# Renumbering the PSUM banks of a fused attention and gated MLP kernel, with a new order of its steps

## The chip, the core and the metric

One NeuronCore of a Trainium2 chip runs the whole program. The metric is device time in microseconds (us) of one execution; the kernel before takes 639.93 us (median of 3 runs, 639.92 to 640.62). Five engines work from queues of their own and meet only at semaphores: TensorE (PE; its weight loads are shown as PEld), VectorE (DVE), ScalarE (ACT), GpSimd (POOL) and SyncE (SP), which issues most DMAs.

## What is computed

For 8 batches and 8 heads (576 positions, head size 64), causal attention by blocks of 64, then a gated MLP over each batch:

```python
scores = q @ k.T / sqrt(64);  scores = where(block_i >= block_j, scores, -1e9)
attn = exp(scores - max);  attn = attn / (sum(attn) + 1e-9);  x = attn @ v      # heads side by side: 576 x 512
h = relu(x @ w_in);  u, v = h[..., :512], h[..., 512:]
v_n = (v - mean(v)) / sqrt(var(v) + 1e-6)
v_s = w_spatial @ v_n + b_spatial
out = (u * v_s) @ w_out
```

Everything is fp32 in and out. Most matmuls are done as three products of rounded parts (high by high, high by low, low by high), so that each fp32 product costs three fast matmuls.

## The kernel before

**Steps.** The program is written as generators that yield after each small piece, a *step*; nearly every step is one instruction on one engine, or one burst of matmuls. A long string, `ORDER` (lines 46 to 155), names which generator is advanced next (`s.17*8` advances the scores of pair 17 eight times). `in_order` (lines 397 to 410) ties each instruction to the one before it on the same engine, so the string fixes the order in every engine's queue; between engines only data and buffers decide.

**Kinds of steps.** Two heads make a pair; there are 32 pairs g, four to a batch b. For each pair: `8.g` (`scores_8`, line 705) computes the scores of the last 64 rows, two PSUM banks, 64 by 64 in the array; DVE reduces each bank with its maximum (line 652, both into the one buffer `p8`), ACT takes the exponential, POOL normalises, `t8.g` (line 839) transposes on DVE. `s.g` (`scores_run`, line 781) computes the other four row tiles t = 3, 2, 1, 0 of both heads in one burst that needs six banks (t = 1 and 0 share one), 64 rows by 128 columns; DVE reduces them (line 593), ACT and POOL follow, `t.g` transposes (line 849, 8 instructions), `r.g` regroups by DMA. `a.g` (`av_pair`, line 882) multiplies with v in two halves z of one bank each, 128 rows by 64 columns; ACT copies each half out (line 506) and DVE subtracts for the low part (line 508), which frees the bank. For each batch the MLP has five `v` groups (12 or 8 matmuls), eight `u`, eight `g` (the spatial product) and fourteen `o` (the output product in seven products of halves), all over the full 128 by 128 array. `h` and the later steps of `g` prepare operands of `o` on ACT and POOL. Pairs 0 to 4 are treated apart in the opening (`set`, `ns`, `ts`, `alo`, `ahi`), where `w` and `sw` also load and split the weights; from `8.5` on the pairs of batch b + 1 run between the MLP groups of batch b.

**PSUM banks.** Eight banks: two (`ps_m`) for `v`, `u`, `g` and `o` with n = 0, six for the pairs: three in pool `s`, two in `t`, one in `av`. `bank` (line 580) picks the pool by a number modulo six, `RING` (line 578), and the pool hands out its buffer that came free first. A pair owns ten numbers: 0 to 5 its `s` banks, 8 and 9 the `8` banks of the next pair, and 6 and 7 the `a` banks of the pair before it (`16 + z` counted from that pair). So the numbers assume the sequence s.(g-1), a.(g-2), 8.g, s.g. The output groups with n = 1 and n = 3 take numbers 4 and 5 of pairs 4b + 7 and 4b + 8, which the scores of these pairs use too.

**Order around the change.** The order before goes to the narrow matmuls of a pair twice, once for `8.g` with both halves of `a.(g-2)` before or behind it, and once, a few wide groups later, for `s.g`.

Of the kernel before, what the change touches and what calls it, by code (L numbers as in the profile page):

```python
# [52 lines left out]
ts.10*2 set.14*2 ns.11 alo.1 ns.11*3 w.4 set.12 ts.10*2 alo.1 ns.12*2 loadv.2 ns.11 ts.9*2
ts.8*2 set.14*3 set.13*5 sw.1 ahi.1 ahi.2*3 w.5 w.6*3 ns.13 set.15*6 ns.13*2 ts.11*4 ns.14*3
ts.12 ahi.2*2 pad ahi.0 load.4 set.16*3 alo.2 loadv.3 set.15*2 ts.12*3 alo.2*2 w.4*3 set.15
ts.13*4 ts.14*4 ns.15*5 load.5 w.5*3 set.16*3 set.17*5 set.18*2 sw.1 ns.16*2 w.6*3 ahi.3*3 ts.15
ahi.2 ts.15*3 ns.17*3 set.19 set.18*3 alo.3*2 ns.16 8.5 set.19*5 ahi.3*3 set.19*3 w.6 w.7*3 t8.4
sw.4*2 alo.3 v.0.0*2 ns.18*3 t8.4 ns.19*3 t.4*3 w.8*3 ns.19 v.0.0*2 load.6 t.4*3 ns.19 t.4*2
# [12 lines left out]
n.8*4 a.7 n.8*5 loadv.8 o.0.3.1 n.8 t8.8*2 r8.8 8.9*3 o.0.4.0*2 o.0.2.1 o.0.4.1 o.0.3.1 o.0.4.1  # L71
a.7*3 8.9*2 o.0.5.0*3 t.8*2 load.10 split.9 o.0.6.0*2 t.8*5 n.8 t.8 r.8 v.1.0*4 o.0.6.1*3 a.5
o.0.5.1*3 a.4 a.7 a.6 v.1.4*2 v.1.0*2 split.9*2 v.1.0*2 8.9*3 s.9*11 v.1.4 v.1.1*2 v.1.4*5
u.1.0.1*2 v.1.1*2 n.9*4 u.1.0.0*2 s.9*5 t8.9*2 n.9*2 s.9 n.9 o.0.6.0 n.9*3 t.9*4 split.10*2 n.9
t.9*4 8.10 a.8*7 v.1.4*3 v.1.2*2 8.10*5 u.1.0.2*2 split.10 v.1.1*4 v.1.3*2 loadv.9 o.0.1.0
v.1.2*3 s.10*5 u.1.0.3*2 8.10*3 v.1.3*3 s.10*3 u.1.1.1*2 s.10*8 v.1.2 u.1.1.0 n.10*6 s.10 n.10*3
r8.9 t8.10*2 load.11 8.11*3 o.0.4.1 v.1.2*2 u.1.1.0 n.10*2 t.10*6 v.1.3*3 r.9 a.9*6 split.11*3
t.10*2 u.1.1.2*2 u.1.1.3*2 g.1.0.0*2 8.11*3 loadv.10 s.11*12 g.1.0.0*2 g.1.0.1*2 r8.10 g.1.0.1*2
o.0.4.0 s.11*5 8.11*3 g.1.0.2*4 load.12 split.12 g.1.1.0*3 n.11*5 g.1.0.3*4 t8.11*2 loadv.11
n.11*6 r.10 a.10*2 split.12*2 a.10*2 t.11*8 8.12 g.1.1.0 g.1.1.1*3 g.1.1.2*7 a.10 8.12*5 a.10  # L80
g.1.1.3*3 o.1.0.1*2 o.1.1.1*2 o.1.0.0*2 o.1.1.0*2 g.1.1.3*6 g.1.1.1 h.1.1 o.1.1.0 s.12*4 load.13
g.1.1.0 r8.11 h.1.0 s.12*9 g.1.1.1 s.12*2 g.1.1.2*2 o.1.2.1*2 o.1.2.0*2 8.12*3 n.12*4 s.12
# [6 lines left out]
s.14*5 u.2.0.3*2 s.14*3 v.2.3*3 n.14*2 v.2.4*3 s.14 n.14 s.14*2 n.14*2 s.14 n.14*4 u.2.1.0
n.14*2 t8.14*2 load.15 8.15*3 t.14*8 u.2.1.0 v.2.2*3 r.13 a.13*6 u.2.1.1*2 v.2.3*3 u.2.1.2*2  # L90
u.2.1.3*2 loadv.15 split.15*3 g.2.0.0*4 8.15*6 g.2.0.1*3 r8.14 g.2.0.1 s.15*9 g.2.0.2*4 n.15*5
s.15*2 g.2.0.3*4 s.15*6 n.15*4 g.2.1.0*3 load.16 split.16*2 8.16 t8.15*2 r.14 a.14*2 o.1.4.0
a.14*2 r8.15 t.15*4 split.16 t.15*2 n.15*2 t.15*2 g.2.1.1*3 g.2.1.2*7 a.14 g.2.1.3*3 o.2.0.1*2
g.2.1.2 o.2.0.0*2 g.2.1.0*2 8.16*5 g.2.1.3*6 o.2.1.1*2 g.2.1.1*2 o.2.1.0*3 a.14 s.16*10 g.2.1.2
o.2.2.0*2 8.16*2 n.16*4 8.16 s.16*6 o.2.1.1 h.2.0*4 o.2.2.1*2 h.2.1*4 o.2.3.0 r.15 a.15*2 t.16
a.15*2 t8.16*2 load.17 8.17*4 a.15*2 o.2.3.1 o.2.4.1 o.2.3.1 o.2.4.1 o.2.3.0 o.2.4.0*2 n.16 s.16
n.16*6 t.16*4 o.2.4.0 t.16*3 8.17*3 o.2.6.1*2 o.2.6.0*2 o.2.5.0*3 loadv.16 load.18 split.17*3
a.13 8.17*2 o.2.5.1*3 v.3.0*4 a.14 s.17*7 r8.16 a.15 a.12 v.3.4*2 s.17*8 loadv.18 o.2.6.1 v.3.1
s.17*2 v.3.4*4 v.3.0*4 u.3.0.0*2 v.3.4*2 n.17*4 t8.17*2 8.18 r.16 a.16*2 n.17*3 v.3.1*3 t.17
split.18 n.17*4 t.17*3 a.16*2 t.17*4 r8.17 u.3.0.1*2 u.3.0.2*2 v.3.4*3 v.3.2*2 8.18*5 split.18*2  # L100
# [1249 lines left out]
```

## Time and profile before

| | |
|---|---|
| median of 3 runs | 639.93 us |
| profiled execution | 640.71 us, its span 638.9 us |
| PE busy | 629.6 us, 99% of the span, 5380 matmuls |
| DVE, POOL, ACT busy | 78%, 67%, 66% |
| granted TensorE clock | 0.999 of full, all 40 slices at 9 tenths or more |

The span runs from the first to the last instruction; the remaining 1.8 us of the profiled execution lie around it. A matmul's end is modelled and matmuls overlap, so PE busy time says that PE is occupied, not how well; the distance from the start of one group to the start of the next says what a group costs. An idle time in brackets at the end of a row is what the engine waited before it, with the instruction that ended the wait.

### The profile page before, as it was taken

The numbers are of one execution on the slowest core, as the hardware profiler recorded it, in microseconds if no ns is written. First come the engines' busy times: TensorE is split into PE (matmuls) and PEld (weight loads), VectorE is DVE, ScalarE is ACT, GpSimd is POOL, SyncE is SP. The second block draws the span as 40 slices with busy tenths as digits, with TensorE's granted clock in tenths as the row PEclk, the third lists the DMA queues.
The fourth block names the chain that finished last, engine by engine and source line by source line (L and its number), as shares of the span: only waits on it lengthen the run. The fifth ranks groups of instructions, "written<-read, shape, count | busy, mean of one in ns | idle before, by whom it ended". The sixth has DMA issues, their size and how long they took to land.

```text
span 638.9 us, 15873 instructions
## 1 busy us (share of the span) xinstructions
PE 629.6 (99%) x5380; PEld 547.2 (86%) x5380; DVE 501.3 (78%) x1847; ACT 424.4 (66%) x1214; POOL 428.6 (67%) x690
## 2 busy tenths in 40 slices
...
PEclk9999999999999999999999999999999999999999
...
GB/s 273 208 130 219 177 133 197 134 147 158 142 175 134 183 162 158 90 206 114 155 205 129 156 159 105 165 194 158 143 81 223 107 208 123 135 123 47 10 1 84
DMA packets 51109, 93.47 MB, mean 146 GB/s; under 512 B 5970, under 2 KB 27986, under 8 KB 51028
## 3 DMA queue, kind: packets, MB, share of 16 engines
...
q14 instruction: 39, 0.32, 0.1%
...
## 4 chain that ended last, share of the span: by engine, by line
PE 87%; DVE 7%; DMA 2%; ACT 1%; POOL 1%; issue 1%; SPq 0%; DVEq 0%; POOLq 0%
PE ms L1082 15%; PE mo L1162 15%; PE mu L1030 14%; PE mv L947 12%; PE av L894 10%; PE s L801 7%; PE s L619 2%; PE av L906 2%; PE mv L959 2%; DMA raw<-qk 2%; DVE p L593 2%; PE t L453 1%; PE ms L1087 1%; PE ms L1086 1%; PE s_first L763 1%
## 5 line engine op out<-in xcount | busy, mean ns | idle before, releaser
L598 ACT ACTIVATE p<-p,sst 128x256 f32<-128x256 f32 (+2 forms) x240 | 132.1, 553 | 14.4 <-DVE sst L593 10.7
L695 POOL TENSOR_SCALAR p<-p,sst 128x256 f32<-128x256 f32 (+4 forms) x244 | 128.0, 543 | 18.3 <-DVE sst L691 4.8
L1030 PE MATMUL mu<-x,wi_hi 128*128 128x288 f32 x512 | 110.2, 299 | 0.6 <-ACT u L1036 0.6
L849 DVE STREAM_TRANSPOSE pb<-p 128x512 f32<-128x512 f32 (+1 forms) x224 | 93.4, 475 | 4.2 <-POOL p L695 3.6
L593 DVE CUSTOM_DVE_ANT_0 p<-s,mask 128x512 f32<-128x512 f32 (+1 forms) x216 | 92.9, 483 | 3.6 <-PE s L801 3.2
L1008 POOL TENSOR_TENSOR vl<-vr,vh 128x512 fp32r<-128x512 f32 x32 | 41.7, 1308 | 77.9 <-ACT vh L1006 57.4
L1030 PEld LDWEIGHTS mu<-x,wi_hi 128*128 128x128 f32 x512 | 84.0, 188 | 5.1 <-ACT p L598 0.9
L947 PE MATMUL mv<-wi_hi,x 128*128 128x512 f32 x256 | 84.1, 394 | 0.0
L1082 PE MATMUL ms<-ws_hi,vh 128*128 128x288 f32 x256 | 77.2, 301 | 0.4 <-DVE u L1090 0.4
L1082 PE MATMUL ms<-ws_hi,vl 128*128 128x288 f32 x256 | 75.6, 295 | 0.0
L1082 PE MATMUL ms<-ws_lo,vh 128*128 128x288 f32 x256 | 75.5, 295 | 0.0
L894 PEld LDWEIGHTS av<-ptt,v 128*64 128x64 f32 x896 | 53.3, 137 | 19.9 <-issue 8.7
L1030 PE MATMUL mu<-x,wi_lo 128*128 128x288 f32 x256 | 69.7, 294 | 0.0
L894 PE MATMUL av<-ptt,v 128*64 128x64 f32 (+3 forms) x896 | 67.5, 303 | 0.0
L947 PEld LDWEIGHTS mv<-wi_hi,x 128*128 128x128 f32 x256 | 48.1, 188 | 10.7 <-issue 0.4
L1062 POOL TENSOR_TENSOR a<-u,a 128x288 fp32r<-128x288 f32 x48 | 38.6, 808 | 27.6 <-ACT a L1058 25.1
L1090 DVE TENSOR_TENSOR u<-ms,u 128x288 f32<-128x288 f32 x64 | 28.8, 451 | 28.8 <-PE ms L1087 23.8
L1082 PEld LDWEIGHTS ms<-ws_hi,vh 128*128 128x128 f32 x256 | 48.4, 189 | 3.1 <-issue 1.3
L947 PE MATMUL mv<-wi_lo,x 128*128 128x512 f32 x128 | 50.0, 391 | 0.0
L1030 PEld LDWEIGHTS mu<-x,wi_lo 128*128 128x128 f32 x256 | 48.1, 188 | 0.5
L1082 PEld LDWEIGHTS ms<-ws_lo,vh 128*128 128x128 f32 x256 | 48.3, 189 | 0.0
L1082 PEld LDWEIGHTS ms<-ws_hi,vl 128*128 128x128 f32 x256 | 48.3, 189 | 0.0
...
## 6 DMA issues: line engine op xcount, KB each, us to landing
ptt<-pb SPq DMA_DIRECT2D x112, 320.0 KB, 6.2
...
ptt<-pb SPq DMA_DIRECT2D x112, 80.0 KB, 2.3
...
```

The source lines that it names most:

```text
L593: nc.vector.tensor_tensor_reduce(out=p, in0=ps, in1=mask[:, 512 - ps.shape[1]:], scale=-0.125, scalar=BIG, op0=ALU.add, op1=ALU.min, accum ...
L598: nc.scalar.activation(p, p, AF.Exp, bias=st[:, k:k + 1], scale=-1.0, accum_out=st[:, 10 + k:11 + k])
L695: nc.gpsimd.tensor_scalar(out=p, in0=p, scalar1=st[:, k:k + 1], scalar2=1.0, op0=ALU.mult, op1=ALU.mult)
L801: mm(ps[(t, hd)], q[js, Q_AT[t]:Q_AT[t] + P], k[js, K0:K0 + n], start=(m == 0), stop=(m == len(of) - 1),)
L849: nc.vector.transpose(to(C_AT[hd][0] + 32 * t, dims), p)
L894: mm(to[js, :, 32 * c:], vt[:, c, js], ptt[:, 2 * z:2 * z + 2, at:at + P - 32 * c], start=(c == 0), stop=(c == 3),)
L947: mm(ps, xs[k][:, j, cs], w[:, k, DH:], start=(n == 0), stop=(n == 3 * NC - 1),)
L1008: nc.gpsimd.tensor_tensor(out=vl, in0=vr, in1=vh.bitcast(F32), op=ALU.subtract)
L1030: mm(ps[:, :HT], w[:, k, ds], xs[k][:, j, zs], start=(n == 0), stop=(n == 3 * NC - 1),)
L1062: engine.tensor_tensor(out=lo, in0=f, in1=hi.bitcast(F32), op=ALU.subtract)
L1082: mm(ps[:, :HT], a[:, ds], w[:, k, zs], start=(n == 0), stop=False)
L1162: mm(ps, y[:, k, es], a[:, k, :], start=(m == 0 and n in (0, 1, 3)), stop=(m == 3 * DQ - 1), skip_group_check=True,)
```

## The change

Three things are changed. `bank` takes a plain number; a new function `visit` numbers the banks of a pair: 0 and 1 for `8.g`, 2 and 3 for `a.(g-2)`, 4 to 9 for `s.g`, and four numbers are inserted between the pairs where a batch ends, for the output groups n = 1 and n = 3, which no longer share numbers with scores. The pools and their sizes are unchanged. And `ORDER` is another string of the same 3257 steps: no instruction is added or removed. The lines of it that are spoken of below are shown with their surroundings.

```diff
-w.1*7 load.0 set.0 sw.2*2 set.0*8 set.1*5 ns.0*5 set.2*5 ns.1*3 w.0*3 set.3*3 ns.2*3 ts.0*4
-load.1 set.4*2 set.3 ns.3*2 ts.1*4 set.4*2 w.0*3 loadv.0 alo.0*2 w.2*2 sw.2*2 w.2 ns.4*2 ts.2*4
...
-n.7*3 s.7*8 n.7*2 loadv.7 w.11*2 n.7*6 g.0.0.3*2 r.6 a.6*4 load.8 split.8 8.8 w.11 t8.7*2 load.9
-t.7*5 split.8 t.7*3 g.0.1.3*3 g.0.1.0*4 g.0.1.2 g.0.1.1*4 split.8 o.0.0.1*2 g.0.1.3 a.6*2 8.8*5
-g.0.1.2*2 g.0.1.3*2 s.8*3 o.0.0.0*2 s.8*4 g.0.1.2*3 s.8*3 g.0.1.2*2 g.0.1.3*3 o.0.1.0*2 r8.7
-8.8*3 g.0.1.2 s.8*7 o.0.1.1 h.0.1*4 8.9 o.0.1.1*2 r.7 a.7*2 o.0.2.1 h.0.0*4 o.0.2.0*2 o.0.3.0*2
...
-t8.13*2 n.13*7 8.14*2 a.12*4 v.2.1*2 u.2.0.1*2 t.13 n.13*3 loadv.13 t.13*3 n.13 t.13*4 8.14*4
-v.2.1*3 split.14 v.2.2*2 a.12*2 v.2.3*2 s.14*5 u.2.0.2*2 v.2.4 v.2.1 v.2.4 8.14*3 r8.13 v.2.2*3
...
+w.1*7 load.0 set.0*9 set.1*5 set.2*5 ns.0*3 set.3*3 ns.0*2 ns.1*3 load.1 set.4*2 sw.1*3 w.0*3
+set.3 set.5*5 ns.2*2 ts.0 ns.2 set.6 ts.0*3 set.4*2 ts.1*4 w.4 ns.3*2 set.6*3 sw.2*2 ns.4*2
...
+w.9*3 w.10*5 u.0.1.3 u.0.0.0*2 s.6*2 v.0.4*4 g.0.0.0 u.0.1.3 8.6*3 w.9*4 loadv.6 s.6*2 g.0.0.0*2
...
+g.0.0.3*2 a.6*4 o.0.0.0*2 8.8 a.6 g.0.1.1*2 g.0.1.2*5 s.8 t.7*8 r.7 g.0.1.3*3 o.0.0.1 o.0.2.1
+o.0.2.0 g.0.1.3 o.0.3.0 g.0.1.0*4 a.6 t8.7*2 r8.7 split.9 8.8*5 s.8*7 loadv.8 g.0.1.1 g.0.1.2
+o.0.2.0 o.0.3.0 g.0.1.3 o.0.2.1 h.0.1*2 o.0.3.1 o.0.1.0 h.0.1*2 o.0.1.1*3 h.0.0 8.8 n.8 8.8
...
+u.2.0.1*2 v.2.2*2 v.2.1*3 t.13 v.2.2*5 v.2.1 v.2.3*2 t.13*6 v.2.2 t.13 r.13 8.14 t8.13 8.14
+t8.13 8.14 a.12*6 v.2.4*3 s.14*2 r8.13 s.14 u.2.0.2 s.14*2 u.2.0.2 u.2.0.3*2 v.2.3*3 v.2.4*3
...
-    def bank(nm, k, b, pr):
-        pool, tag = RING[(10 * (b * NPAIR + pr) + k) % len(RING)]
+    def bank(nm, k):
+        pool, tag = RING[k % len(RING)]
         return pool.tile([P, 512], F32, tag=tag, name=nm)
 
+    def visit(g, k):
+
+        return 10 * g + 4 * max(0, (g - 5) // 4) + k
...
-        ps = [bank(f"s8_{b}_{pr}_{hd}", hd - 2, b, pr) for hd in range(2)]
+        ps = [bank(f"s8_{b}_{pr}_{hd}", visit(b * NPAIR + pr, hd)) for hd in range(2)]
...
-                        bk = bank(f"s{t}_{b}_{pr}_{hd}", 2 * (3 - t) + hd, b, pr)
+                        bk = bank(f"s{t}_{b}_{pr}_{hd}", visit(b * NPAIR + pr, 4 + 2 * (3 - t) + hd))
...
-            av = bank(f"av_{b}_{pr}_{z}", 16 + z, b, pr)
+            av = bank(f"av_{b}_{pr}_{z}", visit(b * NPAIR + pr + 2, 2 + z))
...
-                    kept[n, i] = bank(nm, 4 + i, b + 1, NPAIR - 1 if n == 1 else NPAIR)
+                    kept[n, i] = bank(nm, visit(NPAIR * b + 9, i - 4 if n == 1 else i - 2))
```

## Rows read from the trace of the kernel before

**Rows 1.** The page: busy time by engine, and the granted TensorE clock in 40 slices.
```profile
PE 629.6 (99%) x5380; PEld 547.2 (86%) x5380; DVE 501.3 (78%) x1847; ACT 424.4 (66%) x1214; POOL 428.6 (67%) x690
...
PEclk9999999999999999999999999999999999999999
```

**Rows 2.** Who PE waited for: us in total, times, longest.
```profile
PE s L801 <- DVE x L508: 1.7, 2, 1.0
PE s_first L763 <- DMA raw<-qk: 1.4, 2, 1.1
PE warm L208 <- DVE mask L202: 1.1, 1, 1.1
PE mu L1030 <- ACT u L1036: 0.6, 1, 0.6
PE t L453 <- POOL p L695: 0.5, 1, 0.5
PE ms L1082 <- DVE u L1090: 0.4, 1, 0.4
PE s_first L619 <- DMA raw<-qk: 0.3, 1, 0.3
```

**Rows 3.** PE in order of time: start, us, instructions; into and out of s.13.
```profile
212.29 0.39 PE L947 MATMUL mv<-wi_lo,x 128*128 128x512 f32 x1
212.51 0.39 PE L947 MATMUL mv<-wi_hi,x 128*128 128x512 f32 x1
212.83 0.49 PE L801 MATMUL s<-hi 64*128 64x512 f32 x2
213.17 0.39 PE L801 MATMUL s<-lo,hi 64*128 64x512 f32 x2
213.39 0.39 PE L801 MATMUL s<-hi,lo 64*128 64x512 f32 x2
213.62 0.33 PE L801 MATMUL s<-hi 64*128 64x384 f32 x2
213.79 0.34 PE L801 MATMUL s<-lo,hi 64*128 64x384 f32 x2
...
214.80 0.40 PE L1030 MATMUL mu<-x,wi_hi 128*128 128x288 f32 x1
215.04 0.30 PE L1030 MATMUL mu<-x,wi_lo 128*128 128x288 f32 x1
215.17 0.29 PE L1030 MATMUL mu<-x,wi_hi 128*128 128x288 f32 x1
```

**Rows 4.** PE in order of time: 8.14 with a.12 behind it, then a wide group.
```profile
221.18 0.72 PE L619 MATMUL s<-raw 64*64 64x288 f32 x8
221.83 2.40 PE L894 MATMUL av<-ptt,v 128*64 128x256 f32 x32
...
224.75 0.40 PE L1030 MATMUL mu<-x,wi_hi 128*128 128x288 f32 x1
```

**Rows 5.** PE in order of time: 8.12 with a wide group behind it.
```profile
186.48 0.72 PE L619 MATMUL s<-raw 64*64 64x288 f32 x8
187.13 0.40 PE L1082 MATMUL ms<-ws_hi,vh 128*128 128x288 f32 x1
```

**Rows 6.** PE in order of time: s.6 and s.7.
```profile
83.36 0.92 PE L801 MATMUL s<-raw 64*128 64x384 f32 x4 [0.72 <-DVE x L508]
...
101.96 0.92 PE L801 MATMUL s<-raw 64*128 64x256 f32 x8 [1.03 <-DVE x L508]
```

**Rows 7.** Stretches: length; PE, PEld, DVE, ACT, POOL busy; clock, DMA share, GB/s.
```profile
48.00:64.00 16.00, 16.00 (x97) 12.00 (x94) 14.80 (x60) 14.76 (x41) 14.58 (x23) 1.00 0.77 221
64.00:80.00 16.00, 15.41 (x136) 12.30 (x135) 15.15 (x59) 14.53 (x42) 14.52 (x22) 1.00 0.64 177
80.00:96.00 16.00, 15.28 (x143) 12.83 (x143) 15.46 (x59) 10.93 (x33) 13.42 (x21) 1.00 0.54 133
96.00:112.00 16.00, 14.53 (x133) 12.43 (x133) 15.06 (x52) 8.06 (x25) 14.93 (x27) 1.00 0.76 195
112.00:128.00 16.00, 16.00 (x160) 13.88 (x158) 13.53 (x53) 11.76 (x37) 15.37 (x23) 1.00 0.57 134
128.00:640.00 512.00, 507.73 (x4426) 455.79 (x4421) 388.72 (x1414) 323.58 (x924) 322.33 (x517) 1.00 0.53 137
```

**Rows 8.** DVE in order of time: t8.7, t.7, then a.6 and 8.8.
```profile
110.71 0.89 DVE L839 STREAM_TRANSPOSE pb<-p 128x320 f32<-128x320 f32 x2
111.53 3.22 DVE L849 STREAM_TRANSPOSE pb<-p 128x512 f32<-128x512 f32 x8
...
116.72 0.44 DVE L652 CUSTOM_DVE_ANT_0 p<-s,mask 128x288 f32<-128x288 f32 x1
```

**Rows 9.** POOL in order of time: what o.0.2.1 needs (s2l).
```profile
121.63 0.80 POOL L1062 TENSOR_TENSOR s2l<-s,s2h 128x288 fp32r<-128x288 f32 x1
...
123.14 0.80 POOL L1062 TENSOR_TENSOR s2l<-s,s2h 128x288 fp32r<-128x288 f32 x1
```

**Rows 10.** PE in order of time: o.0.2.1.
```profile
124.02 0.40 PE L1162 MATMUL mo<-s2h,wo_t_hi 128*128 128x288 f32 x1
```

**Rows 11.** DVE in order of time: the two reductions of 8.14.
```profile
224.72 0.43 DVE L652 CUSTOM_DVE_ANT_0 p<-s,mask 128x288 f32<-128x288 f32 x1
...
229.05 0.42 DVE L652 CUSTOM_DVE_ANT_0 p<-s,mask 128x288 f32<-128x288 f32 x1
```

**Rows 12.** ACT and DVE groups by line: the copies and reductions that free banks.
```profile
L506 ACT CAST x<-av 128x256 fp32r<-128x256 f32 (+1 forms) x68 | 24.6, 382 | 18.2 <-PE av L906 10.0 <-PE av L894 5.6 <-DMA outT<-o 1.3
L508 DVE TENSOR_TENSOR x<-av,x 128x256 fp32r<-128x256 f32 (+1 forms) x68 | 26.8, 426 | 0.7 <-ACT x L506 0.5
```

**Rows 13.** PE in order of time: t = 2 of s.21, behind o.3.6.0.
```profile
366.30 0.42 PE L801 MATMUL s<-hi 64*128 64x384 f32 x2
366.56 0.33 PE L801 MATMUL s<-lo,hi 64*128 64x384 f32 x2
```

More of the change, by code (lines that the diff above doesn't have):

```diff
@@ L53 @@
[L53 to L58, printed above, removed]
@@ L71 @@
[L71 to L76, printed above, removed]
@@ L77 @@
[L77 to L82, printed above, removed]
@@ L89 @@
[L89 to L94, printed above, removed]
@@ L95 @@
[L95 to L100, printed above, removed]
@@ new lines @@
+set.3 set.5*5 ns.2*2 ts.0 ns.2 set.6 ts.0*3 set.4*2 ts.1*4 w.4 ns.3*2 set.6*3 sw.2*2 ns.4*2
+ns.5*3 loadv.0 alo.0 ts.2*4 ts.3*2 loadv.2 set.7*2 alo.0*2 set.6 ns.6*3 w.2*3 ts.3*2 set.7*4
+sw.3 set.7*3 ahi.0*3 w.4 w.0*3 w.4 w.0 ns.7*5 ts.6*4 w.2*3 ahi.0*2 load.2 w.2 set.8*4 ts.5*4
+ns.8*2 ts.4*4 set.10*5 set.9*5 w.4*2 load.3 ts.7*4 ns.9 ns.10*2 loadv.1 ahi.1 w.3*3 set.11*3
+ts.8*2 ns.9*2 w.3*4 set.11*5 set.12*3 w.5*2 alo.1*3 set.13*2 set.12 ns.12 set.11 ns.11 ts.9*4
+ahi.1*4 set.14 ts.10*2 w.5 ns.10 ts.10*2 ns.12 set.13*3 ns.11*4 set.14 pad set.14*2 ts.8*2
@@ new lines @@
+ts.11*2 w.4*2 ns.13 ahi.0 ns.13*2 w.6*2 set.14 ns.14*3 ahi.2*5 w.6 set.15*8 ahi.1 ahi.2 set.15
+load.4 set.16*3 sw.2*2 ts.13*2 set.16 ts.13*2 ts.11 ts.12*2 ts.11 set.17 set.16 ns.15*3 set.16
+ts.12*2 ns.15*2 sw.1 w.5*4 ts.14*4 sw.3 set.17*2 alo.2*2 set.17*2 set.18*5 ns.16 ns.17*3 ns.16*2
+alo.2 sw.0*2 w.6*2 sw.3*2 ts.15*3 load.5 loadv.3 ahi.3*5 ts.15 sw.4*2 set.19*4 8.5 w.7 set.19*4
+t.4 ns.18*3 alo.3*3 set.19 sw.4 loadv.5 ns.19*3 w.8 t8.4*2 t.4*2 w.7*2 load.6 r8.4 8.5 v.0.0*4
+sw.4 ns.19*2 w.6*2 w.8*2 sw.0*2 v.0.2*2 loadv.4 w.7*2 8.5*4 w.7*2 v.0.1*2 v.0.0*4 w.9 ahi.3
@@ new lines @@
+o.0.4.1 8.9*3 a.7 load.10 a.7*3 o.0.5.0*3 o.0.6.0*2 a.6 o.0.6.1*2 n.8 o.0.6.1 o.0.5.1*2 8.9*3
+t.8*3 n.8 t.8*3 n.8 t.8 n.8 t.8 r.8 o.0.5.1 o.0.6.0 v.1.0*4 s.9*4 8.9*3 v.1.4*5 split.10*3
+v.1.1*2 s.9*3 u.1.0.0 s.9 u.1.0.0 s.9*4 v.1.0 u.1.0.1 v.1.0*3 v.1.1*2 n.9*3 u.1.0.1 load.11
+s.9*2 n.9 s.9*3 t8.9*2 r8.9 v.1.2*2 8.10*3 t.9 8.10 a.8*4 n.9*7 v.1.2*3 a.8*2 o.0.1.0 v.1.4
+t.9*5 8.10*2 t.9*2 v.1.2*2 r.9 v.1.2 v.1.4 split.11*3 v.1.4 s.10*2 u.1.0.2*2 v.1.3*2 v.1.1*3
+u.1.0.3*2 v.1.3*3 u.1.1.0*2 v.1.1 a.8 loadv.10 s.10*7 v.1.4 8.10 n.10*3 8.10*2 v.1.4*2 s.10*8
@@ new lines @@
+u.1.1.2*2 t8.10*2 r8.10 n.10*3 v.1.3*3 u.1.1.1 loadv.11 u.1.1.1 load.12 8.11*4 n.10*4 t.10*3
+a.9*7 u.1.1.3*2 t.10*3 n.10 t.10*2 r.10 8.11*3 g.1.0.0*4 g.1.0.2*4 s.11*6 load.13 8.11*2
+g.1.0.1*4 split.12*3 g.1.1.0*2 s.11*4 n.11*2 g.1.0.3*4 s.11*7 n.11*2 o.0.4.0 n.11*7 g.1.1.1*3
+t8.11*2 r8.11 g.1.1.2*2 g.1.1.0 g.1.1.2*3 t.11*8 a.10*4 o.0.4.1 g.1.1.2*4 8.12*3 r.11 8.12*3
+a.10*2 g.1.1.3*4 loadv.12 g.1.1.0*2 o.1.0.1*2 s.12*6 o.1.0.0*2 g.1.1.3*5 g.1.1.1*2 8.12 n.12
+8.12*2 h.1.1 o.1.1.1*3 load.14 o.1.1.0*2 o.1.2.1*2 o.1.2.0*2 n.12*2 a.10 h.1.1*3 h.1.0*4
@@ new lines @@
+u.2.1.0*2 a.12 8.14*3 u.2.1.1*2 split.15 s.14*7 8.14*3 n.14*6 s.14*5 t8.14*2 r8.14 split.15*2
+loadv.15 v.2.3*3 n.14*4 u.2.1.2*2 t.14*6 n.14 t.14*2 u.2.1.3*2 load.16 a.13*6 r.14 g.2.0.0*4
+g.2.0.1*4 8.15*6 loadv.14 s.15*6 a.13 8.15 n.15*2 8.15*2 split.16*2 g.2.0.2*2 o.1.4.1 g.2.0.2*2
+s.15*4 g.2.0.3*3 n.15*4 split.16 g.2.1.0*3 g.2.0.3 s.15*7 n.15*5 g.2.1.1*3 g.2.1.0 g.2.1.2*5
+t.15*6 o.1.1.0 t.15*2 g.2.1.3*4 g.2.1.2*2 g.2.1.3 load.17 r.15 g.2.1.0 t8.15*2 r8.15 a.14*4
+g.2.1.1*2 h.2.0 8.16*6 load.18 g.2.1.3*4 loadv.18 a.14*3 o.2.0.0*2 g.2.1.2*2 o.2.0.1*2 s.16*6
@@ new lines @@
+o.2.1.0*2 h.2.1 o.2.1.0 o.2.1.1*2 o.2.2.1*2 s.16*3 8.16 n.16 o.2.2.0*2 h.2.1*2 o.2.3.1*2 h.2.0*3
+s.16*5 o.2.4.1*2 o.2.3.0*2 o.2.4.0*2 loadv.16 s.16*3 o.2.5.1*3 split.17 h.2.1 o.2.6.1*3 8.16
+t8.16 8.16 t8.16 r8.16 o.2.4.0 n.16*3 o.2.4.1 n.16*4 o.2.6.0*3 o.2.5.0*3 8.17*4 split.17*2
+a.15*5 n.16*2 a.15*2 8.17*2 t.16*7 n.16 t.16 r.16 s.17*4 8.17*3 v.3.0*3 v.3.4*5 v.3.0 split.18
+loadv.17 u.3.0.0*2 s.17*8 v.3.1*2 n.17*2 s.17*2 n.17*2 s.17*3 v.3.1*2 u.3.0.1*2 v.3.0*4 v.3.1*3
+n.17*4 t8.17*2 r8.17 n.17*2 load.19 n.17 v.3.1 t.17*2 v.3.2*3 8.18 v.3.2*2 t.17*3 a.16*4 8.18*3
@@ new lines @@
+v.3.4 t.17*3 split.18*2 u.3.0.2*2 a.16*2 8.18*2 v.3.2*2 u.3.0.3*2 v.3.2 r.17 load.20 v.3.4*5
+v.3.3*5 s.18*2 split.19*3 u.3.1.2*2 v.3.3*3 u.3.1.0*2 a.16 s.18*3 8.18 n.18*3 s.18*4 8.18*2
+s.18*4 n.18*3 u.3.1.3*2 g.3.0.0*3 t8.18 g.3.0.0 s.18 t8.18 r8.18 a.17*7 8.19*6 s.18*3 t.18*2
+u.3.1.1*2 g.3.0.1*3 n.18*4 loadv.19 t.18*5 n.18 t.18 r.18 split.20*2 s.19*6 g.3.0.1 g.3.0.2*4
+load.21 8.19 n.19*2 8.19*2 g.3.0.3*4 s.19*11 g.3.1.0*3 g.3.1.1*3 split.20 n.19*7 g.3.1.2*5
+o.3.0.0*2 t.19*6 n.19 t.19 n.19 t.19 g.3.1.3*4 r.19 g.3.1.2*4 t8.19*2 r8.19 a.18*6 o.2.1.1
@@ new lines @@
+8.20*3 o.3.0.1*2 g.3.1.3*5 s.20*6 g.3.1.0*2 s.20*2 g.3.1.1*2 o.3.1.0*3 o.3.1.1*2 load.22 h.3.1*3
+8.20*4 n.20 h.3.0*4 o.3.2.1*2 o.3.3.1*2 o.3.2.0*2 o.3.3.0 s.20*6 a.19*2 o.3.4.1*2 o.3.4.0
+o.3.3.0 o.3.4.0*2 h.3.1 o.3.6.1*3 n.20*4 loadv.20 s.20*3 o.3.6.0*2 n.20 o.3.6.0 t.20*3 8.20*2
+t8.20*2 r8.20 n.20*3 o.3.5.0*3 split.21*3 a.19*4 n.20 8.21*2 o.3.5.1*3 v.4.0*2 t.20*4 n.20 t.20
+r.20 8.21*2 s.21*6 v.4.0 a.18 s.21*2 v.4.0*2 loadv.21 a.19 v.4.4*2 8.21*2 v.4.4*2 split.22*2
+8.21*3 n.21*3 v.4.1*3 s.21*6 n.21 s.21*3 v.4.4*2 split.22 t8.21*2 r8.21 u.4.0.0*2 u.4.0.1*2
```

122 lines of the change are left out of this document (52 added, 70 removed).

## The prediction, made before the changed kernel was run

> **What bounds the kernel now.** I read the busy time by engine first: TensorE is occupied for 629.6 of 638.9 us, at a granted clock of 0.999 [rows 1]. So time can only come from what TensorE waits, or from bursts that cost more than they need. The list of its waits is next [rows 2]: 5.0 us in nine waits, of which 1.1 at the warming matmuls and 1.7 for the first loads stay as they are. The others are four pairs of engines: 1.7 us in which a burst of scores waits for DVE's subtraction on an a half, that is for a PSUM bank; 0.6 for ACT, 0.5 for POOL, 0.4 for DVE. By place [rows 7], all of this lies before 112 us; from 128 to 640 us TensorE misses 4.3 of 512 us, 3.2 of them behind its last matmul. So the main part has no wait to win, and only the number of times that TensorE changes its shape is left there. The same rows show that the opening is not TensorE's alone: from 48 to 112 us DVE is busy 60.5 of 64 us and POOL 57.5, from 112 to 128 us POOL 15.4 of 16. What is taken from TensorE's waits there has to be found on DVE and POOL too.
>
> **Part 1: fewer changes of shape.** No instruction is added or removed; bursts change neighbours. I wrote out the tensor bursts of both strings and counted neighbours of different shape (wide; 64 by 64 for 8; 128 by 64 for a; 64 by 128 for s). Before: 37 up to 8.5 and 140 from there, 177. After: 36 and 135, 171. Ten times s.g now stands right behind a.(g-2) or 8.g, which takes one change out each time; elsewhere four come back, since an a loses its 8 or is split (a.19, a.23).
> Price of one [rows 3]: between two v matmuls 0.22 us pass, between the last and the first of s.13 0.32; the first pair of s.13 takes 0.34, the second 0.22. That is 0.10 + 0.12. On the way out the first u matmul takes 0.24 against 0.13 for the next, 0.11, with about as much ahead of it as on the way in. So 0.2 us a change, and 6 x 0.2 = 1.2 us saved. Nothing hides it, as TensorE is the bound. Bounds: 0.1 (entry alone) gives 0.6, 0.25 gives 1.5.
> A shape change inside a visit is not free either: 8.14 with a.12 behind it lasts from 221.18 to 221.83 [rows 4], and 8.12 with a wide group behind it from 186.48 to 187.13 [rows 5], 0.65 us both. The Trainium skill (TensorEngine Tiling (Array Packing), Key Properties) says that changing the tiling mode, not just the tile, drains TensorE; these two rows agree with 0.65 us. It speaks against counting visits: there are 58 before and 51 after, and at two changes each this would be 7 x 0.4 = 2.8 us saved; by changes it is 1.2.
>
> **Part 2: the waits for banks of a.** s.6 stops 0.72 us before its t = 2 tiles and s.7 1.03 before t = 1 [rows 6]. By the old numbers the banks of a.(g-2) (6 and 7) come back as t = 2 (12 and 13 are 0 and 1 of the ring again, two places on), and in s.7 as t = 1, since 8.7 was issued ahead of a.5. By the new ones t = 2 gets the banks of 8 and t = 1 those of a. For s.6 this alone is some 0.9 us later, and one more u group (1.6 us) stands between a.4 and s.6; for s.7 a.5's six steps now stand in one piece, ahead of t.6. Both waits go: -1.7 us (bounds -1.7 and 0).
>
> **Part 3: the other waits of the opening.** POOL 0.5 us: before ts.0 there are now set.4 and set.5, and load.1 is two loads earlier on SP's queue. ACT 0.6 and DVE 0.4: other groups stand there. I take -1.0 of 1.5 (bounds -1.5 and +1.0, as ts.0 and the whole chain of exponentials behind it starts later).
>
> **Part 4: what the opening gives back.** Two places. First 8.8: the new string has a.6 twice, o.0.0.0, 8.8, s.8 on TensorE, and on DVE a.6's first subtraction, all of t.7, a.6's second, t8.7, and only then 8.8's reductions. Three banks of pool s are taken by 8.8 and t = 3 of s.8, so t = 2 must wait for the first reduction. From the end of a.6's first half: ACT 0.38 and DVE 0.43 [rows 12] with two handovers of 0.1, 1.0; then 3.2 + 0.4 + 0.9 + 0.4 [rows 8] = 4.9; free at 5.9. TensorE arrives after the second half 1.8 (half of the 2.9 in [rows 4] and two changes), the o group 0.9 (six matmuls of 0.13), 8.8 0.65 and t = 3 0.8 (as in s.13, [rows 3]): 4.1. A wait of 1.8 us, and queued behind it are s.8 and all later bursts. Second, o.0.2.1 now stands 3.6 us of tensor work earlier (8.9, half of a.7, o.0.1.0 and o.0.1.1 come behind it). It needs both s2l: before they end at 122.4 and 123.9 [rows 9] and o.0.2.1 starts at 124.0 [rows 10], just in time. In the new string POOL has 1.2 us less in front of them (without two of g.0.1.0 and one of g.0.1.1, 2.4; with a.4's copy and one more of g.0.1.2). If POOL keeps its pace, o.0.2.1 starts at about 122.8, with 3.6 us more to do behind it: 2.4 us given back, net. POOL idled 6.5 us of 64 before 112 [rows 7], and sw.3 and w.8 now stand earlier, so I expect half of that. The two places overlap (a wait at 8.8 is one less at o.0.2.1), so +1.3 us, between 0 and 3.3.
>
> **Part 5: tight banks in the main part.** In ten places a burst now follows directly on what frees its bank, and four times o.b.1.0 takes the bank that t = 3 of s has just left. Each is met if DVE is free within some 0.3 us: behind s, the reduction of t = 3 ends about 1.7 us after the start, and o starts at 2.0. Such places of before cost little: in s.21 t = 2 waits for o.3.6.0, and its first pair takes 0.26 against the 0.17 of s.13 [rows 13, 3]. But 8.14's reductions ended 3.9 and 8.2 us after its burst began [rows 4, 11], which the spacing of before allows. With 14 x 0.05 I take +0.7 (bounds 0 and 14 x 0.4 = 5.6).
>
> **Sum.** -1.2 - 1.7 - 1.0 + 1.3 + 0.7 = -1.9 us on the profiled execution of 640.7, 638.8. The median lies 0.8 lower, so 639.9 - 1.9 = 638.0 us.
>
> **Rivals.** (A) The forecast, about 638.0, from 637.2 to 638.6. (B) The opening was held by order, not by DVE and POOL: parts 1 to 3 in full and nothing back, 639.9 - 1.2 - 1.7 - 1.5 = 635.5. For it: POOL and ACT have room before 48 us. Against it: DVE's 60.5 of 64 us. (C) The opening is DVE's and POOL's: what TensorE no longer waits at s.6 and s.7 it waits at s.8 and o.0.2.1. Parts 2 to 4 sum to nothing, part 1 and part 5 leave -0.5: 639.4. For it: [rows 7] and the just-in-time s2l. (D) Slower: DVE is late at the bank handovers of the merged visits. Place: t = 2 and t = 1 of s.10, s.14, s.15, s.17, s.23, s.25, s.27, s.29, s.30, and o.b.1.0. Price: for each us that DVE lags beyond 0.3, almost a us a place; at a lag of 0.6 in the 14 places 4.2 us, with the 1.8 of s.8 and without part 3: 639.9 - 1.2 - 1.7 + 1.8 + 4.2 = 643.0. It decides from a mean lag of about 0.4. For it: the reductions of 8.14; against it: the new string puts the reductions of 8 and the subtractions of a right behind their bursts, ahead of the transposes, everywhere but at 8.8.
>
> **How the numbers follow.** A 0.36, B 0.12, C 0.32, D 0.20. About 0.2% (1.3 us) is what a measurement of this kernel tells from no change. Faster is A and B: 0.48. Of C and D, C and a little of D lie within 0.2%: 0.34. Slower is the rest of D, 0.18. The range leaves out the far end of D and a tip of B: 635.4 to 641.8; the likeliest case alone 637.2 to 638.6.
>
> **What would show it.** Right: 171 changes at 0.2 us; no wait of s on L508 before 104 us; a wait of s.8 of about 1.8 us for L652, and o.0.2.1 not before s2l; TensorE's idle time from 128 us on below 5 us. Wrong: waits of s bursts for L652, L593 or L508 in most visits (D); no wait at s.8 at all (my order on DVE is not what binds); idle time of the opening as large as before (C).

## The result: 644.5 us, 0.8% slower, and the profile after

The changed kernel takes 644.47 us (median of 17 executions, 641.29 to 648.82) beside 639.92 for the kernel before (17, 639.3 to 641.0); the ratio is 1.0078, 95% interval 1.006 to 1.0096. The prediction was 638.0, faster, with a range from 635.4 to 641.8. The scatter is new too: 7.5 us where the kernel before has 1.7. The profiled execution took 643.13 us (span 641.3), 2.4 more than that of before and 1.3 less than its own median. Code behind the new function lies 3 lines further down than before (L801 is L804, L652 is L655), code ahead of it 1 line further up (L208 is L207); in some of the runs further below they are shifted by one more.

From the page after, busy time by engine and the granted clock in 40 slices; they answer to [rows 1]:

```profile
PE 631.8 (99%) x5380; PEld 549.9 (86%) x5380; DVE 503.8 (79%) x1847; ACT 424.0 (66%) x1214; POOL 436.8 (68%) x690
...
PEclk9999999999999999999999999999999899999999
```

TensorE is as full as before, but in slice 32 the granted clock has fallen. Who it waited for (us in total, times, longest), beside [rows 2]:

```profile
PE mo L1165 <- ACT s L1177: 2.7, 1, 2.7
PE s L804 <- DVE sst L655: 1.7, 2, 1.5
PE warm L207 <- DVE mask L201: 1.1, 1, 1.1
PE mo L1165 <- DVE sst L596: 0.5, 1, 0.5
```

The waits of the opening that the prediction wanted gone are gone: L508 (1.7), ACT (0.6), POOL (0.5), DVE (0.4). So are, but for 0.2, those for the first loads (1.7), which it had put down as staying. One wait of s for a reduction of `8` has come (1.5), and two of output groups, for ACT (2.7) and for DVE (0.5), that the list of before doesn't have. The stretches, beside [rows 7]:

```profile
48.00:64.00 16.00, 16.00 (x94) 11.59 (x92) 14.59 (x58) 13.90 (x38) 15.85 (x24) 1.00 0.70 204
64.00:80.00 16.00, 15.92 (x147) 13.87 (x144) 14.96 (x56) 15.39 (x41) 14.91 (x21) 1.00 0.56 151
80.00:96.00 16.00, 16.00 (x149) 13.75 (x148) 15.43 (x61) 11.93 (x36) 15.52 (x25) 1.00 0.58 161
96.00:112.00 16.00, 16.00 (x149) 14.35 (x147) 14.31 (x49) 6.18 (x20) 15.75 (x25) 1.00 0.69 184
112.00:128.00 16.00, 14.55 (x148) 12.31 (x149) 12.56 (x47) 13.31 (x41) 15.16 (x24) 1.00 0.59 135
```
```profile
496.00:504.00 8.00, 5.10 (x37) 4.87 (x37) 4.30 (x18) 4.84 (x15) 4.92 (x7) 1.00 0.81 189
504.00:512.00 8.00, 8.00 (x56) 7.58 (x58) 4.98 (x18) 4.33 (x16) 6.80 (x11) 0.79 0.45 169
```

TensorE now idles 0.1 us from 48 to 112 us where it idled 2.8. At 100.6 us the changed kernel has 363 tensor groups left; the kernel before had 364 left at 102.8, one of 2.0 us more: the kernel before was 4.2 us behind at equal work. Of this s.8 gives back 1.7 (1.45 of it the wait at 116 us, below), the groups behind it win 1.0 again, so 3.5 are left at 128 us. Not all of this is the change's. At the first `v` matmul the changed kernel is 1.3 us ahead (51.88 against 53.20), but two runs below that have the order of before up to there (num_only 52.29, main_new 52.25) are 0.9 ahead of the same profile: it had waited long for its first loads. So the change has won about 2.6. I then summed, group by group, the distance from one start to the next in both traces: from 128 to 480 us they differ by 0.1 us, from 480 to 512 us by 6.0, from there on by nothing. The whole loss is at s.28 and the output groups of batch 5 behind it.

**How these 6 us come about.** TensorE in order of time (the idle time in brackets):

```profile
494.31 0.44 PE L804 MATMUL s<-hi 64*128 64x384 f32 x1 [0.29 <-DVE sst L655]
...
496.15 0.40 PE L1165 MATMUL mo<-a,wo_hi 128*128 128x288 f32 x1 [0.49 <-DVE sst L596]
...
503.98 0.41 PE L1165 MATMUL mo<-dh,wo_t_hi 128*128 128x288 f32 x1 [2.75 <-ACT s L1177]
...
505.11 0.44 PE L1165 MATMUL mo<-dh,wo_t_hi 128*128 128x288 f32 x1
505.35 0.44 PE L1165 MATMUL mo<-dh,wo_t_lo 128*128 128x288 f32 x1
```

The last two rows are 0.24 us apart, where such matmuls took 0.13 [rows 3]: behind the gap the granted clock was at the lower of its two levels (1.2 against 2.4 GHz) for part of the stretch, 0.79 on average, which cost 1.6 us over the three groups concerned. So 1.3 at s.28 (waits of 0.29 and 0.49, and its banks in single file), 2.8 at o.5.4.1, 1.6 by the clock, 0.3 in other groups. Back along the chain, ACT first (ACTq is its queue issuing a DMA):

```profile
498.38 0.19 ACT L601 ACTIVATION_READ_ACCUMULATOR p<-p,sst 128x1 f32 x1
501.27 0.34 ACTq L1189 DMA_DIRECT2D outT<-o  x1
501.72 0.94 ACT L383 CAST hi<-raw 128x896 fp32r<-128x896 f32 x1 [3.16 <-PE mo L1165]
...
503.23 0.69 ACT L1177 COPY s<-mo 128x288 f32<-128x288 f32 x2
```

The two copies that o.5.4.1 waits for stand behind a store, o.5.1.0's, that ACT issues only at 501.27, though its data was ready by 498.56. What the store waits for is in the list of the built program's instructions, not in the view of waits (which names PE for the idle time): a semaphore of DVE, for that data, and a semaphore of a DMA. The program has eight such semaphores, used in turn by the transfers of SP and of ACT. The one before on this semaphore is the third of r.27's regrouping, and the store must wait until that has landed; it was issued at 493.69 and landed at 501.19. SP issued r.27 late:

```profile
492.45 5.06 SPq L880 DMA_DIRECT2D ptt<-pb  x4
497.56 4.32 SPq L872 DMA_DIRECT2D ptt<-pb  x4
```

because DVE's transposes of t.27 were late, behind one subtraction:

```profile
485.95 2.90 DVE L386 TENSOR_TENSOR lo<-raw,hi 128x512 fp32r<-128x512 f32 x1
488.77 2.73 DVE L852 STREAM_TRANSPOSE pb<-p 128x512 f32<-128x512 f32 x6
```

Its 24 instances have a median of 0.72 us; this one took 2.90. POOL over the same time:

```profile
485.96 0.81 POOL L1108 TENSOR_TENSOR u<-u 128x288 f32<-128x288 f32 x1
486.74 0.81 POOL L1065 TENSOR_TENSOR a<-u,a 128x288 fp32r<-128x288 f32 x1
487.50 0.80 POOL L1123 TENSOR_TENSOR s<-u 128x288 f32<-128x288 f32 x1
488.38 1.13 POOL L1126 TENSOR_TENSOR u<-s,u 128x288 f32<-128x288 f32 x1
```

POOL runs three instructions back to back; at the first gap, 488.30, DVE gets its turn, ends 0.55 later, and now POOL's fourth takes 1.13 for 0.81. Read so, the two engines exclude each other here. The Trainium skill (SBUF — State Buffer, Who interferes with whom) says that DVE instructions with two SBUF inputs (against a GpSimd instruction that reads SBUF), or in a two-port mode, contend with GpSimd for one pair of ports, and that whoever issues first has it for the whole instruction. The rows agree as to the exclusion, and they go further: DVE lost not one turn but three in a row.

### The profile page after: what moved, and what is told of

The parts are those of the page before. It is cut to its first block, busy times and chain, and to the rows that moved or that the text cites. A ratio compares the mean times of both kernels' runs of the same rounds, so it can differ in the third digit from the quotient of the medians.

```text
span 641.3 us, 15865 instructions
## 1 busy us (share of the span) xinstructions
PE 631.8 (99%) x5380; PEld 549.9 (86%) x5380; DVE 503.8 (79%) x1847; ACT 424.0 (66%) x1214; POOL 436.8 (68%) x690
## 4 chain that ended last, share of the span: by engine, by line
PE 91%; ACT 4%; DVE 2%; DMA 2%; issue 1%; SPq 0%; POOL 0%; ACTq 0%; DVEq 0%; POOLq 0%
PE ms L1085 16%; PE mu L1033 16%; PE mo L1165 14%; PE mv L950 12%; PE av L897 10%; PE s L804 8%; PE s L622 3%; PE av L909 2%; PE mv L962 2%; PE s_first L766 2%; PE t L452 1%; PE ms L1090 1%; PE ms L1089 1%; DMA ptt<-pb 1%; ACT p L601 1%; PE s_first L738 1%
## 5 line engine op out<-in xcount | busy, mean ns | idle before, releaser
L698 POOL TENSOR_SCALAR p<-p,sst 128x256 f32<-128x256 f32 (+3 forms) x244 | 131.0, 555 | 28.7 <-DVE sst L694 20.5
L852 DVE STREAM_TRANSPOSE pb<-p 128x512 f32<-128x512 f32 (+1 forms) x224 | 93.6, 476 | 2.9 <-POOL p L698 1.5
L596 DVE CUSTOM_DVE_ANT_0 p<-s,mask 128x512 f32<-128x512 f32 (+1 forms) x216 | 94.2, 481 | 1.8 <-PE s L804 1.3
L676 POOL TENSOR_SCALAR p<-p,sst 128x288 f32<-128x288 f32 x56 | 30.4, 554 | 30.5 <-DVE sst L647 25.6
```

The source lines that it names most:

```text
L596: nc.vector.tensor_tensor_reduce(out=p, in0=ps, in1=mask[:, 512 - ps.shape[1]:], scale=-0.125, scalar=BIG, op0=ALU.add, op1=ALU.min, accum ...
L698: nc.gpsimd.tensor_scalar(out=p, in0=p, scalar1=st[:, k:k + 1], scalar2=1.0, op0=ALU.mult, op1=ALU.mult)
L852: nc.vector.transpose(to(C_AT[hd][0] + 32 * t, dims), p)
```

## The experiments

Two theories of the first four runs were mine before these rows were traced to the end (P: one place; B: bank waits everywhere), a third was the clock (C). L, the lock between DVE and POOL, came from their traces. In the diffs `-` and `+` are parts of the order of the changed kernel and of the experiment; `...` stands for steps left out.

**The store later.**
```diff
-... o.5.1.0*3 o.5.1.1*2 split.29 h.5.1*3 o.5.2.0*2 o.5.2.1*2 load.30
+... o.5.1.0*2 o.5.1.1*2 split.29 h.5.1*3 o.5.2.0*2 o.5.2.1*2 o.5.1.0 load.30
```


> The changed kernel with one step moved: the store of o.5.1.0 (an output DMA issued by ACT) stands behind the two sums copies of o.5.2.0 and o.5.2.1 instead of ahead of them. Theory P (one place): in the changed kernel ACT stood from 498.6 to 501.2 us at this store, until a transfer of r.27 had landed, and o.5.4.1 waited 2.75 us for the copies behind it; the granted clock then fell to 0.79 over 8 us, 1.6 us more. Without it that wait is under 0.3 us, the clock 0.999, and the median 644.5 - 4.4 = 640.1. Theory B (bank waits of the new numbers everywhere, my rival D): this place is one of many, the median stays at 643 to 645. Theory C (the granted clock falls in some executions by itself): the wait goes, but clock and times scatter as before, 641 to 649.

641.95 us (12 executions), ratio 1.0031 (1.0011 to 1.005): 2.5 less than the changed kernel. The times fall in two groups, six from 638.8 to 640.7 and six from 643.2 to 645.4. The profile is of the second group:

```profile
PE mu L1033 <- ACT vr L956: 1.8, 1, 1.8
PE s L804 <- DVE sst L655: 1.7, 2, 1.5
...
PE mu L1033 <- DVE st L986: 1.0, 1, 1.0
PE mo L1165 <- DVE o L1186: 0.9, 1, 0.9
```

The wait of 2.75 is gone; the output group behind o.5.4.1 waits 0.9 for DVE in its place. But 2.8 us of waits for u stand at 69 and 72 us that the profile of the changed kernel, with the same order there, doesn't have. I compared the two traces instruction by instruction: they part at one DVE instruction, L264, the decoding of weight block w.7. In the changed kernel, then here:

```profile
56.65 0.66 DVE L264 SCALAR_TENSOR_TENSOR r_gl<-r_gl 128x512 int32<-128x512 int32 x1
```
```profile
56.75 3.69 DVE L264 SCALAR_TENSOR_TENSOR r_gl<-r_gl 128x512 int32<-128x512 int32 x1
```

And POOL in the changed kernel, then here (three instructions in the first row of each):

```profile
55.73 1.73 POOL L698 TENSOR_SCALAR p<-p,sst 128x128 f32<-128x128 f32 x3
57.43 1.45 POOL L325 TENSOR_TENSOR wi_lo<-r_gh,wi_hi 128x256 fp32r<-128x256 f32 x2
```
```profile
55.76 1.17 POOL L698 TENSOR_SCALAR p<-p,sst 128x128 f32<-128x128 f32 x3
56.90 1.46 POOL L325 TENSOR_TENSOR wi_lo<-r_gh,wi_hi 128x256 fp32r<-128x256 f32 x2
58.31 1.59 POOL L325 TENSOR_TENSOR ws_lo<-rs,ws_hi 128x288 fp32r<-128x288 f32 x2
60.54 0.64 POOL L316 TENSOR_SCALAR wi_hi<-r_gl 128x512 fp32r<-128x512 f32 x1 [0.64 <-DVE r_gl L264]
```

Once DVE began 0.11 us behind POOL's third instruction, and that one was stretched by 0.55; once it began 0.19 behind it and stood back behind five POOL instructions, 3.0 us. A race of 0.1 us decides over 3. That it makes the two groups is a reading: no profile of the faster group was taken. So theory P held for the place, but not for the time (640.1), which only the faster group has; B was not needed; theory L was formed here. C is not gone: the granted clock over an execution still differs, 0.995 to 1.0. But in the traces of all these runs each of its nine falls ahead of the last matmul stands at a wait of TensorE (1.59 to 2.77 us), so it does not fall just anywhere. Nor does the length of the wait decide: it fell behind 1.60 us in the run lo_early, not behind 2.56 in the run lose (both below):

```profile
120.00:128.00 8.00, 8.00 (x56) 7.78 (x53) 3.26 (x14) 6.52 (x19) 6.55 (x10) 0.80 0.79 187
```
```profile
504.00:512.00 8.00, 5.66 (x42) 5.32 (x44) 4.61 (x17) 6.21 (x20) 6.26 (x9) 1.00 0.62 197
```

**The new numbers with the order of before.**


> The new numbering of the banks with the order of before. Theory P: the numbers by themselves do little, 639 to 641, with other short waits of a or s in the opening. Theory B: the new numbers cost waits for reductions in the main part, 642 or more. Theory C: times scatter by 4 us or more.

649.31 us (5 executions), 1.0155 (1.0142 to 1.0169), all within 1.7 us. P's claim that the numbers do little by themselves is wrong, and B's is right (642 or more):

```profile
PE av L898 <- DVE sst L597: 4.8, 3, 2.0
PE s L623 <- DVE sst L597: 2.2, 2, 1.2
```

In the old sequence `a` now gets banks that s has just filled, and waits for their reductions. The new numbers need the new order. The new order with the old numbers was not run, so how much of the gain in the opening needs the new numbers stays open.

**The new opening with the old main part, and the reverse** (joined where v.1.0 begins; 4 of some 830 steps change sides).


> The changed kernel up to step 831 (about 130 us), then the remaining steps in the order of before; new numbers throughout. From the two traces the new opening is 3.5 us ahead at 128 us, the wait of s.8 included. Theory P: 639.9 - 3.5 = 636.4, no wait over 0.5 us behind 130 us. Theory B: the old main part with new numbers gives back 2 us or more, 638.5 to 642. Theory C: scatter of 4 us or more about that.

> The steps of before up to step 827 (about 132 us), then the remaining steps in the new order; new numbers throughout. Theory P: opening as before, then the loss at s.28 to o.5.4.1 (6.0 us in the profile, which lies 1.3 us under the median): 639.9 + 6.0 = 645.9, up to 648; one wait over 2 us near 500 us. Theory B: the same time, but with waits spread over the merged visits. Theory C: as the changed kernel, 641 to 649, with the drop of the clock at another place than 500 us.

650.87 us (1.0172, 1.0158 to 1.0185) and 649.26 us (1.0149, 1.0136 to 1.0162). Both carry a half in which the new numbers meet the old order, so neither tells what I built it for, and no theory's range has either time (P: 636.4, and up to 648). The second shows the wait at o.5.4.1 again, 2.4 us at 512.8, behind another opening: it belongs to the main part.

**DVE's subtraction earlier.**
```diff
-s.27*5 loadv.27 g.5.0.1*4 ... split.28 t.27*6 ...
+s.27*5 loadv.27 g.5.0.1 split.28 g.5.0.1*3 ... t.27*6 ...
```


> The changed kernel with one step moved: DVE's half of the low part of pair 28 (lo <- raw, hi: 128x512, both inputs in SBUF) stands some 8 us earlier on DVE, ahead of the product of g.5.0.1, where POOL is idle, and not ahead of t.27. Theory L (lock): in the changed kernel this instruction took 2.90 us against 0.72 as the median of its 24, as long as POOL ran four instructions back to back beside it; that made t.27, r.27, the store of o.5.1.0 and o.5.4.1 late. Now it takes 0.7, no wait of PE from 485 to 515 us, granted clock 0.999 there, median 644.5 - 5 = 639 to 640. Rival S (the store and its DMA semaphore alone): DVE's instruction is no cause, PE still waits over 2 us at o.5.4.1, median 643 to 645.

642.29 us (12 executions), 1.0037 (1.0012 to 1.0062); again two groups, 638.8 to 640.9 and 643.7 to 647.7, and a profile of the second. The subtraction is no longer lengthened (0.69), both waits at s.28 are gone, and that of o.5.4.1 is 1.5 instead of 2.75. So L is right on the cause of half of it; the store's semaphore (S) keeps the other half. The median lies in neither's range (639 to 640, 643 to 645): the race in the opening, which this run still has, is in it.

**The race out.**
```diff
-... w.6*2 w.8*2 sw.0*2 v.0.2*2 loadv.4 w.7*2 8.5*4 ...
+... w.8*2 v.0.2*2 loadv.4 w.7*2 w.6*2 sw.0*2 8.5*4 ...
```


> The changed kernel with four POOL steps (the low parts of w.6 and sw.0) moved behind w.7 in the opening, near 57 us, so that POOL has no string of instructions ready while DVE decodes w.7 (L264, both inputs in SBUF). Theory L: this one instruction took 0.66 us in the profile of the changed kernel and 3.7 us in two other profiles with the same opening, after a start 0.1 us later; that is the scatter of 3 to 4 us between executions. Now it takes under 1.2 us in all: the waits of u at 69 and 72 us (1.8 and 1.0) are not there, and the times lie within 3 us of each other, median 642 to 643.5. Rival C (the granted clock falls by itself): scatter of 641 to 649 as before.

643.33 us (5 executions, 642.0 to 644.8), 1.0055 (1.0043 to 1.0068). The decoding takes 0.66, no wait of 0.1 us stands at 69 or 72 us, and the group above 646 is gone, as L says, though with five executions that alone could be chance (6 of the changed kernel's 17 lie there).

**The reverse: the race always lost, with two inputs and with one.**
```diff
-... loadv.4 w.7*2 8.5*4 w.7*2 ...
+... loadv.4 8.5 w.7*2 8.5*3 w.7*2 ...
```
The run with one input has in addition, for block w.7, `tensor_scalar(out=low, in0=high, ...)` in place of `scalar_tensor_tensor(out=low, in0=high, ..., in1=low, ...)`.

> The changed kernel with one step swapped near 57 us: the first reduction of 8.5 stands ahead of w.7's decoding (L264, both inputs in SBUF) on DVE, so that this instruction always begins some 0.6 us later, while POOL is already in its string of four. Theory L: it takes over 2.5 us in every execution, u waits 1.5 us or more at 69 and 72 us, and all executions lie where the slow half of the changed kernel lies, 645 to 649, median 647. Rival C: times as the changed kernel, 641 to 649, median 644.5, whatever this instruction takes.

> The same order, but w.7's decoding on DVE has one input in SBUF instead of two (it leaves out the low bits of that block of weights). Theory L, where the second input is what needs POOL's port: it takes under 0.8 us beside the same string of POOL, no waits over 0.3 us at 69 and 72 us, 641 to 645, median 643 to 644. Rival A (any DVE instruction started inside a string of POOL is held): 3 us as with two inputs, median 647.

646.73 us (6 executions; five from 646.5 to 648.0, one of 643.99), 1.0101 (1.0085 to 1.0117), and 644.74 us (644.1 to 647.2), 1.0076 (1.0061 to 1.0091). The decoding in the one and the other:

```profile
56.91 3.43 DVE L264 SCALAR_TENSOR_TENSOR r_gl<-r_gl 128x512 int32<-128x512 int32 x1
```
```profile
57.67 3.09 DVE L265 TENSOR_SCALAR r_gl<-r_gl 128x512 int32<-128x512 int32 x1
```

The first is as L says for the decoding in its profile. The one time below L's range, 643.99, is the profiled execution itself, so there too the decoding was held. What sets it apart is the clock: 0.999 granted over the execution, against 0.997 and 0.994 in the five slower ones. With one input it is the same, 0.999 at 644.07 to 644.27 and 0.994 at 647.20, so the 2.0 us between the two medians go with the clock and say nothing about the decoding. The second refutes my version of L: one input from SBUF is held as two are. In all traces with the new opening it goes together: where the decoding took 3.1 us or more (six), TensorE waited 1.2 us or more for u at 69 to 70 us; where it took 0.8 or less (five), not over 0.2. Nor is it every DVE instruction (rival A): in the traces of before and after, none of the 280 transposes of L839 and L849 (L842 and L852 after) took over 0.72 us, nor any of the reductions of L652 (0.46), though POOL ran beside most of them. The Trainium skill's rule on two-port modes (SBUF — State Buffer, Who interferes with whom) would cover such a single-input instruction. That it ran in one no run here shows outright; it ended 0.28 us behind POOL's last instruction of the string, the one with two inputs 0.55, so once free it was about twice as fast.

**s.8's wait.** Twice: the reductions of 8.8 and a.6's second subtraction moved ahead of part of t.7.


> The changed kernel with the two reductions of 8.8 and the second subtraction of a.6 moved ahead of the last two transposes of t.7 on DVE. My step of part 4 (t = 2 of s.8 waits for the first reduction of 8.8, which stands behind t.7): the wait of 1.45 us at 116 us goes to under 0.2, median 644.5 - 1.4 = 643.1. Rival (the opening is DVE's: what s.8 does not wait, a.7 or o.0.2.1 waits, as r.7 is 1.3 us later): 644 to 645.

> The three edits together with the store of o.5.1.0 behind the sums copies. Theory L with my step on s.8: all three losses go, opening 3.5 + 1.4 us ahead of the kernel before, main part level with it: 639.8 - 4.9 = 635, between 634.5 and 637, and a scatter under 3 us. Rival C: 638 or more with a scatter of 6 us.

> As the kernel with three moves, and also t8.7, the first two reductions of 8.8 and the second subtraction of a.6 ahead of the last three transposes of t.7 on DVE (8.8's reductions write the buffer that t8.7 reads, so t8.7 moves with them). My step of part 4: the wait of s.8 (1.5 us) goes, 635.6 to 636.5. Rival (the opening is DVE's): the wait comes back at o.0.2.1 and a.7, at least 1.0 us of 1.5, and the time is that of the three moves within 0.6 us.

In the first two runs (the second with the other three edits) 8.8 overwrites `p8` before t8.7 has read it, so part of the result is 8.8's instead of 8.7's; the work is the same. 646.25 us (1.0092, 1.0068 to 1.0115), 638.17 (0.997, 0.9958 to 0.9982): the first above both forecasts, the second above L's range and no faster than the same without this move (637.92, next run). In the third t8.7 moves along: 639.37 us (12 executions), 0.9997 (0.9985 to 1.0009), 1.5 more than without. The waits in its profile, which is of its slowest execution (643.53, the others 638.5 to 640.8):

```profile
PE av L898 <- DMA ptt<-pb: 1.8, 1, 1.8
...
PE mo L1166 <- ACT o L1174: 0.7, 1, 0.7
PE av L910 <- DMA ptt<-pb: 0.5, 1, 0.5
...
PE s L805 <- DVE sst L656: 0.2, 1, 0.2
```

1.45 us at s.8 become 0.2, and 3.0 come back at o.0.2.1 and a.7, as r.7 left later. The rival is right that the wait comes back, though more than it said (its range was 0.6 us about the time of the three moves). Moved in these two ways the wait brings nothing; that no order could save it is not shown.

**The three moves together** (store, subtraction, race).


> The changed kernel with the three moves of the runs before: the four POOL steps behind w.7, DVE's low part of pair 28 earlier, the store of o.5.1.0 behind the sums copies. Theory L (lock): all executions have the opening without the waits at 69 and 72 us and the main part without those at s.28 and o.5.4.1; only the wait of s.8 (1.5 us) stays. 643.1 - 6.0 = 637.1, median 637 to 638.5, all executions within 3 us of each other, granted clock 0.999 or more. Rival C (the granted clock falls by itself): 640 and more with a scatter of 6 us.

637.92 us (5 executions, 637.2 to 638.3), 0.9963 (0.9952 to 0.9975): 1.9 us faster than the kernel before, and 6.6 faster than the changed kernel. What TensorE waited for:

```profile
PE s L805 <- DVE sst L656: 1.5, 1, 1.5
PE warm L208 <- DVE mask L202: 1.0, 1, 1.0
PE s_first L767 <- DMA raw<-qk: 1.0, 2, 0.7
```

Nothing is left at s.28 or o.5.4.1: r.27 is issued at 490.6 for the same s.28, and the copies run at 498.2 instead of 503.2. It beats both kernels, and L's forecast (637 to 638.5, within 3 us, clock 0.999 or more) holds in every part.

## Why the prediction was wrong, step by step

- **Part 1, changes of shape (-1.2)** and **part 5, tight banks (+0.7)**: -0.5 together, measured level (0.1 us from 128 to 480 us). In the traces TensorE changes its shape 184 times before and 179 after, so five fewer, not six. Behind v.1.0 four changes go, 0.8 us by the price of 0.2, which no run tests by itself; the tight places take 0.6: s.10, s.27 and s.29 cost 0.17 to 0.18 each (2.14 us instead of 1.97 from start to start), s.14, s.15, s.17, s.23, s.25, s.30 and those of o.b.1.0 up to 0.04. At s.27 and s.29, which follow directly on their `8`, the second bank of t = 2 comes free only with the second reduction, 0.4 us behind the first.
- **Part 2, banks of a (-1.7)**: right, both waits of L508 are gone.
- **Part 3, other waits of the opening (-1.0)**: -1.4; all three are gone but for 0.13.
- **Part 4, given back (+1.3)**: right on s.8, in place and cause (1.45 us for L655, estimated at 1.8), and its working holds: t8.7 must come first. Wrong on o.0.2.1, which waits for nothing; in sum 1.45. That this is near 1.3 is luck: the working has 1.8 for s.8 alone, and half of 2.4 with an overlap that it does not price.
- **The step that failed** is the first paragraph's "the main part has no wait to win", read as: none to lose but at banks; with it part 5's "Each is met if DVE is free within some 0.3 us". At s.28 DVE was 2.2 us late, by POOL, and what then ended last was not a bank but ACT, held by a store whose DMA semaphore hung on r.27. My rival D had s.28 among its places, through o.5.1.0, and its 643.0 is near the result, but by luck: at most 1.3 of the 6.0 us came by its mechanism. "TensorE's idle time from 128 us on below 5 us" was the sign that showed it: 6.7.
- **The fall of the clock** (1.6 us behind the gap) I had not priced at all: some waits of TensorE have a second price. And I had no term for **scatter**. The profile of before can't show a race that its order doesn't have, but it does show the exclusion: one of its 24 subtractions (median 0.69) took 1.63, and ended 0.55 behind POOL's second instruction:

```profile
339.26 1.63 DVE L387 TENSOR_TENSOR lo<-raw,hi 128x512 fp32r<-128x512 f32 x1
```
```profile
338.56 0.81 POOL L1105 TENSOR_TENSOR u<-u 128x288 f32<-128x288 f32 x1
339.32 1.02 POOL L387 TENSOR_TENSOR lo<-raw,hi 128x384 fp32r<-128x384 f32 x1
```

- The sum without these, 638.0, is what the kernel with the three moves takes (637.9), in part because the errors cancel: parts 1 and 5 brought 0.5 less than forecast, part 3 brought 0.4 more. The change has, in addition, three collisions that no part of mine looked for.
- Two readings were wrong without harm: the nine waits of [rows 2] add up to 6.0 us, not 5.0, and 8.14's reductions ended 4.0 and 8.3 us after its burst began, not 3.9 and 8.2. A third had a price: the 1.7 us for the first loads do not "stay as they are" from one execution to the next (0.2 in the profile after, 1.0 with the three moves), which lent the opening 0.9 us in the comparison of the two profiles.
